# Linear attention and a multiplicative FFN on one core: another order of the steps, with the fold products begun in pairs

## The chip, the cores and the metric

One core of a Trainium2 chip runs the program. The metric is the device time of one execution in microseconds. Five engines work side by side, each on its own list of instructions in program order: TensorE (PE; its weight loads are shown apart as PEld), VectorE (DVE), ScalarE (ACT), GpSimd (POOL) and SyncE (SP). Transfers run in DMA queues. In this kernel GpSimd and SyncE issue nearly all of them; only the very last is issued by ScalarE.

## The reference, cut to what matters

```python
B, H, S, D = 8, 8, 576, 64              # q, k, v: float32

def phi(x):
    return np.where(x > 0, x, np.exp(x) - 1.0) + 1.0
q_p, k_p = phi(q), phi(k)
kv  = np.einsum('bhsd,bhse->bhde', k_p, v)
z   = np.sum(k_p, axis=2)
num = np.einsum('bhsd,bhde->bhse', q_p, kv)
den = np.einsum('bhsd,bhd->bhs', q_p, z)[..., None] + 1e-06
x   = (num / den).transpose(0, 2, 1, 3).reshape(4608, 512)

a = x @ w1                              # w1, w2: 512 x 1024
b = x @ w2
h = (a * b) @ w3                        # w3: 1024 x 1024
out = h @ w_out                         # w_out: 1024 x 512
```

## The kernel before

**Stages.** The kernel first folds the two last weights into one, wf = w3 @ w_out (eight row blocks i of 128; each is a sum of eight products of 512 columns, kc = 0 to 7). Then the attention runs batch by batch and fills xt, the transposed x, in bf16. The 4608 tokens are nine chunks c of 512. For each chunk eight column blocks f of a and b are computed (four products each, accumulated in PSUM), ScalarE copies a to SBUF, VectorE multiplies it with b to ab, and four products O of 128 tokens (eight matmuls of 512 columns each, against wf) give the output rows. Batches 0 and 1 use a path on TensorE alone for the transposes (q transposes and "first" products), batches 2 to 7 transpose q and x with DMAs of SyncE.

**The order.** Everything is a step in one text, `ORDER` (lines 19 to 68), and `step` (L486) carries the steps out one after the other under a manual schedule. The order in the text is therefore the order on each engine. Waits between engines follow from the data, and from the buffers of the pools: a new tile of a full pool waits until the oldest tile's last reader is done. A "+" at the end of a step puts it on the other engine: a copy on VectorE where it is on ScalarE otherwise, a load in GpSimd's queue where it is in SyncE's otherwise.

| step | what it does | line |
|---|---|---|
| lq, lk, lv b.part | load q, k or v of batch b (part 2: the whole of it) | L165 |
| lw x.y | load a piece of w1 (x = 0) or w2 (x = 1) | L171 |
| lo x | load a quarter of w_out: the rows for kc = 2x and 2x+1 | L181 |
| le i | load block i of w3 | L191 |
| i0, i1, i2, i3 | identity; ones and constants; zero tile; zeros into kvb, on GpSimd | L137 to L147 |
| H n | n products of the zero tile, into a PSUM tile of mm_ps | L152 |
| wt i, wc i | eight transposes of w3's block i on TensorE; their copy out | L202, L206 |
| wm i.k0.k1 | the fold products kc = k0 to k1-1 of block i | L212 |
| wd i | copy of the finished block into wf_sb | L216 |
| x, y, z with k or q | exp (ACT), linear part (DVE) and minimum (DVE) of phi | L226 to L237 |
| vc, K, kc, Z, kz | v's cast, k'v products and their copies, sums of k | L243 to L361 |
| T b.u | q's transpose as a DMA of SyncE | L274 |
| A, G, D | products q kv, their division (DVE), x's transpose as a DMA of SyncE | L286 to L320 |
| qa, qb, e, er, em, rm, rd | the same for batches 0 and 1 without DMA | L330 to L415 |
| g c.f.w.h | products of a (w = 0) or b (w = 1) of chunk c, block f; h = 2: all four kc, 0 or 1: one half | L428 |
| fc, fm c.f | copy of a (ACT), product a * b (DVE) | L439, L448 |
| O, oc c.m | output products of 128 tokens; their copy to an o_sb buffer | L456, L460 |
| S c.m | the store of that buffer, two DMAs of 128 KB (64 tokens each); GpSimd, for chunk 8 SyncE | L468 |
| Q 8.3 | the last output block in two parts, with copies and stores | L479 to L481 |

PSUM has four accumulators of the tag mm (fold products, a, b and O, L117) and two of the tag at (transposes, attention). The copies of O share six o_sb buffers:

```python
        o_sbs[c, m] = sm.tile([P, DM], F32, tag="o_sb", name="o_sb", bufs=6)
        copy_of(alt)(out=o_sbs[c, m], in_=o_pss[c, m])
```

so a copy oc waits until the store of the sixth oc before it has landed. In the text a store S stands some steps behind its copy; in between, the buffer is taken.

The front of the text before, to the first fold products, and the place where chunk 2's output products stand:

```
i2 lq0.0 H12 le3 le0 i0 le4 le1 lo1 xq0.0 yq0.0 lo0 lo2 wt3 lo3 H3 lk0.0+ wt0 le6 wc0+ lk0.1+ wc3+ wt4 zq0.0
le2 wt1 wc4+ lq0.1+ wc1+ qa0.0 le5 wm1.0.4 wm3.0.4 lk1.1+ wm4.0.4 le7 wm3.4.8 wm4.4.8 xk0.0 yk0.0 wm0.0.4
...
fm2.3 fm2.0 S0.1 G3.1 O2.2 oc1.3 D3.0 O2.1 oc2.2 vc5.0+ D3.1 vc4.1 yq4.1 lq5.2 O2.0 oc2.1 zq4.0 S2.2 vc4.0
```

Of the kernel before, what the change touches and what calls it, by code (L numbers as in the profile page):

```python
# [24 lines left out]
e0.1.1 kz0.0.0+ K0.1 er0.1.1 e0.0.0 kz0.0.1+ wm7.0.4 em0.0.0 wm7.4.8 em0.0.1 er0.1.0 wd5+ rm0 lw1.2 e0.1.0
g0.5.0.0 wd7 em0.1.1 g0.4.0.0 rd0 lv1.0+ em0.1.0 g0.0.0.0 g0.1.0.0 g0.0.0.1 lv1.1+ g0.5.0.1 fc0.0 g0.1.0.1
fc0.5 g0.6.0.0 lq2.2+ g0.6.0.1 fc0.1 yk1.0 g0.1.1.0 fc0.6 g0.1.1.1 lv2.2+ g0.4.0.1 xk1.0 fm0.1 g0.2.0.0
g0.2.0.1 fc0.4 g0.7.0.0 zk1.0 lk2.2+ g0.7.0.1 xq1.0 zk1.1 g0.0.1.0 g0.3.0.0 yq1.0 g0.3.0.1 fc0.7 g0.0.1.1
zq1.0 xq1.1 Z1.0 Z1.1 fm0.0 qa1.0 fc0.3 g0.3.1.0 qb1.0+ kz1.1.1 g0.2.1.0 kz1.1.0 g0.3.1.1 yq1.1 fc0.2 e1.0.1
g0.2.1.1 er1.0.1 zq1.1 g0.4.1.0 g0.5.1.0 fm0.2 g0.5.1.1 er1.0.0 fm0.3 g0.4.1.1 g0.7.1.0 fm0.5 g0.7.1.1 qa1.1  # L30
fm0.7 g0.6.1.0 qb1.1 g0.6.1.1 fm0.4 K1.0 fm0.6 K1.1 kz1.0.0 e1.1.1 kz1.0.1 e1.0.0 O0.3 er1.1.1 em1.0.1
em1.0.0 er1.1.0 e1.1.0 oc0.3+ O0.0 em1.1.1 S0.3 xq2.0 em1.1.0 g1.1.0.0 xq2.1 lk3.2 yq2.1 g1.7.0.0 g1.4.0.0
yq2.0 oc0.0 g1.7.0.1 g1.4.0.1 zq2.1 g1.1.0.1 fc1.4 g1.4.1.0 zq2.0 fc1.7 g1.7.1.0 g1.7.1.1 vc2.0+ T2.1 fc1.1
rm1 vc2.1 g1.1.1.0 fm1.7 g1.1.1.1 yk2.0 g1.3.0.0 xk2.1 T2.0 g1.3.1.0 fm1.1 g1.3.0.1 g1.4.1.1 yk2.1 fc1.3
g1.6.1.0 rd1 g1.0.0.0 fm1.4 lq3.2 g1.3.1.1 g1.0.0.1 xk2.0 fm1.3 lv3.2 g1.6.1.1 g1.6.0.0 zk2.1 fc1.0 g1.6.0.1
g1.0.1.0 zk2.0 fc1.6 lk4.2 g1.5.0.0 fm1.6 K2.0 K2.1 g1.0.1.1 kc2.1 kc2.0+ g1.5.1.0 fm1.0 A2.0 A2.1 g1.2.1.0
G2.0 g1.2.0.0 g1.5.0.1 g1.5.1.1 fc1.5 g1.2.1.1 g1.2.0.1 fm1.5 D2.0 A2.3 fc1.2 A2.2 O0.2 yq3.1 xq3.1 fm1.2
xk3.0 G2.1 O0.1 O1.1 oc0.1 yk3.0 D2.1 xk3.1 zq3.1 O1.2 lq4.2 xk4.1 oc1.1+ zk3.0 xq3.0 A2.4 yq3.0 g2.4.0.2
yk3.1 lv5.2 g2.5.0.2 fc2.4 zq3.0 g2.5.1.2 fc2.5 G2.2 T3.1 oc1.2 g2.7.0.2 oc0.2 yk4.1 g2.4.1.2 fc2.7 vc3.0+
# [5 lines left out]
T4.0 fc3.1 zk5.0 g3.4.0.2 vc5.1+ g3.3.0.2 fc3.4 S2.0 xq5.1 fm3.4 g3.5.0.2 yq5.1 g3.2.0.2 S2.3 fc3.5 yq5.0
g3.1.1.2 xq5.0 zq5.1 D2.2 g3.5.1.2 fm3.1 S1.2 K4.0 K4.1 fm3.5 fc3.2 g3.0.1.2 kc4.0 kc4.1+ fc3.3 zq5.0 A4.1
A4.0 g3.2.1.2 G4.0 T5.0 g3.0.0.2 g3.3.1.2 fm3.2 K5.0 D4.0 K5.1 fm3.3 fc3.0 g3.6.1.2 S1.3 kc5.0 fm3.0 A4.2
g3.7.1.2 kc5.1+ S2.1 A4.3 fm3.7 g3.6.0.2 T5.1 G4.1 fc3.6 g4.2.0.2 g4.2.1.2 fc4.2 lv6.2 g4.5.0.2 fm4.2 lq6.2
g4.3.0.2 fm3.6 fc4.5 g4.0.0.2 fc4.3 lk6.2 O3.1 fc4.0 A5.0 oc3.1+ O3.0 A5.1 oc3.0 g4.1.0.2 G5.0 S3.1 g4.5.1.2
vc6.0 D4.1 g4.0.1.2 fm4.5 g4.3.1.2 fm4.0 fc4.1 D5.0 g4.6.0.2 xq6.1 fm4.3 A4.4 g4.6.1.2 G4.2 fc4.6 g4.7.1.2  # L50
xq6.0 yq6.0 O3.3 lq7.2 yq6.1 xk6.0 fm4.6 g4.1.1.2 lk7.2 xk6.1 oc3.3+ A5.4 O3.2 fm4.1 S3.3 G5.2 D4.2 g4.7.0.2
oc3.2 zq6.0 g5.7.0.2 vc6.1+ fc4.7 g5.4.0.2 yk6.1 fc5.7 A5.2 D5.2 fm4.7 fc5.4 g4.4.0.2 zq6.1 g4.4.1.2 fc4.4
zk6.1 T6.1 xq7.0 g5.3.0.2 fm4.4 g5.3.1.2 xq7.1 yq7.0 O4.2 T6.0 yq7.1 fc5.3 zq7.0 xk7.1 O4.3 fm5.3 S3.2 oc4.2
yk7.1 xk7.0 S4.2 zq7.1 g5.7.1.2 zk7.1 oc4.3 g5.2.0.2 S4.3 fm5.7 g5.2.1.2 fc5.2 yk7.0 g5.6.0.2 S3.0 fm5.2
g5.5.1.2 fc5.6 zk7.0 lv7.2 g5.4.1.2 yk6.0 A5.3 g5.0.0.2 fm5.4 T7.1 zk6.0 O4.1 fc5.0 G5.1 T7.0 g5.0.1.2
g5.5.0.2 fm5.0 K6.0 fc5.5 oc4.1+ K6.1 D5.1 g5.6.1.2 kc6.1 fm5.5 kc6.0 S4.1 g5.1.1.2 vc7.0 fm5.6 A6.2 A6.3
vc7.1 g5.1.0.2 G6.1 O4.0 fc5.1 fm5.1 D6.1 A6.0 K7.0 K7.1 oc4.0+ O5.1 kc7.0 S4.0 kc7.1 A6.1 oc5.1 O5.3 G6.0
S5.1 O5.0 oc5.3+ D6.0 A7.4 oc5.0+ A7.1 S5.3 O5.2 G7.2 S5.0 A7.0 oc5.2 g6.4.0.2 G7.0 D7.2 g6.3.1.2 fc6.4 S5.2
g6.0.0.2 D7.0 g6.1.0.2 fc6.0 g6.0.1.2 fc6.1 g6.4.1.2 fm6.0 g6.2.0.2 fm6.4 g6.1.1.2 fc6.2 g6.6.1.2 fm6.1
g6.3.0.2 g6.7.0.2 fc6.3 fm6.3 g6.2.1.2 fc6.7 g7.2.0.2 fm6.2 g6.6.0.2 fc7.2 g7.7.0.2 fc6.6 fm6.6 g7.3.0.2  # L60
fc7.7 g7.2.1.2 g6.7.1.2 fm7.2 g7.6.1.2 fc7.3 fm6.7 g6.5.1.2 g7.6.0.2 g7.4.0.2 fc7.6 fm7.6 g7.7.1.2 fc7.4
g6.5.0.2 fm7.7 g7.3.1.2 fc6.5 fm6.5 g7.0.1.2 fm7.3 O6.1 O6.0 oc6.1+ S6.1 A7.3 oc6.0 g7.4.1.2 S6.0 g7.0.0.2
fm7.4 A6.4 fc7.0 O6.2 G6.2 fm7.0 D6.2 A7.2 g7.5.0.2 oc6.2+ g7.1.0.2 G7.1 S6.2 fc7.5 g7.5.1.2 fc7.1 g7.1.1.2
fm7.5 D7.1 O6.3 fm7.1 O7.2 oc6.3+ S6.3 g8.4.0.2 oc7.2 g8.3.0.2 S7.2 fc8.4 g8.7.0.2 fc8.3 g8.3.1.2 fc8.7
# [534 lines left out]
```

## Time and profile before

| | |
|---|---|
| time, median of 3 runs | 245.5 us (244.54 to 245.67) |
| the profiled execution's own time | 244.84 us |
| its span in the profile | 243.1 us |
| TensorE busy | 232.2 us, 96% of the span |
| VectorE, ScalarE, GpSimd busy | 148.9, 118.4 and 60.2 us |
| moved by DMA | 49.20 MB, 202 GB/s over the span |

The profile comes from one execution. Its span begins with the first and ends with the last recorded work, and the rest of that execution's own time, 1.74 us, lies around it. A row names the engine, the line, the instruction and the tiles it writes and reads (out<-in); times are in us, with the time from the span's start first where a row tells of one instruction. "<-" gives what released the engine after an idle time. The page divides the span into 40 slices; TensorE's row there begins with 8, 5 and 7, ends with 3, and is 9 in all slices between.

### The profile page before, as it was taken

To read this page: it belongs to the slowest core of one execution; us is meant where nothing else is said; L and a number is where in the kernel's file an instruction comes from. 1 tells how busy PE (TensorE), PEld (TensorE's weight loads), DVE (VectorE), ACT (ScalarE), POOL (GpSimd) and SP (SyncE) were. 2 spreads that over 40 slices of the span, in tenths; PEclk is the share of its full clock that TensorE was granted. 3 is DMA by queue.
4 is the path that set the end of the run, shared out by engine and by line. 5 is a ranking of instruction groups with operands and counts; after the bars stand their busy time and mean duration, and the time that the engine had idled before them with its cause. 6 is when DMAs were issued, how large, how long until landed. Compare 5 with 4: busy or idle time off the path is not lost.

```text
span 243.1 us, 4808 instructions
## 1 busy us (share of the span) xinstructions
PE 232.2 (96%) x1938; PEld 112.1 (46%) x1955; DVE 148.9 (61%) x280; ACT 118.4 (49%) x177; POOL 60.2 (25%) x104
## 2 busy tenths in 40 slices
...
GB/s 151 194 283 325 213 255 296 294 387 299 186 395 200 370 263 332 205 272 275 105 256 381 216 373 152 293 122 151 155 119 1 0 3 86 97 86 46 43 79 137
DMA packets 48470, 49.20 MB, mean 202 GB/s; under 512 B 30528, under 2 KB 34880, under 8 KB 48448
## 3 DMA queue, kind: packets, MB, share of 16 engines
...
q8 instruction: 15, 0.25, 0.4%
q10 hardware_dynamic: 144, 0.10, 0.1%
...
## 4 chain that ended last, share of the span: by engine, by line
PE 89%; DMA 4%; DVE 2%; ACT 1%; POOL 1%; issue 1%; POOLq 0%
PE b_ps L428 25%; PE o_ps L456 25%; PE a_ps L428 24%; PE wf_ps L212 6%; DMA wo<-in_moe_w_out_dram 4%; PE nd L286 3%; PE kvp L261 2%; POOL w3b L191 1%; PE w3p L202 1%; PE o_ps L479 1%; PE nd L372 1%; PE tq L330 1%; PE zp L349 1%; DVE k L237 1%; DVE ab L448 1%
## 5 line engine op out<-in xcount | busy, mean ns | idle before, releaser
L428 PEld LDWEIGHTS <-w_sb 128*128 128x128 bf16 x576 | 54.9, 98 | 63.9 <-issue 1.4
L468 POOL DMA_DIRECT2D out_dram<-o_sb x64 | 36.3, 571 | 157.1 <-ACT o_sb L460 72.8
L428 PE MATMUL b_ps<-xt,w_sb 128*128 128x512 bf16 x288 | 70.7, 379 | 0.0
L428 PE MATMUL a_ps<-xt,w_sb 128*128 128x512 bf16 x288 | 69.5, 379 | 0.4 <-DVE xt L392 0.3
L439 ACT COPY a_sb<-a_ps 128x512 f32<-128x512 f32 x72 | 41.7, 585 | 57.6 <-PE a_ps L428 41.6
L456 PE MATMUL o_ps<-wf_sb,ab 128*128 128x512 bf16 x266 | 63.2, 379 | 0.8 <-issue 0.2
L448 DVE TENSOR_TENSOR ab<-a_sb,b_ps 128x512 bf16<-128x512 f32 x64 | 45.8, 730 | 27.7 <-PE b_ps L428 17.8
L456 PEld LDWEIGHTS <-ab 128*128 128x128 bf16 x280 | 26.7, 98 | 31.0 <-issue 0.5
L460 ACT COPY o_sb<-o_ps 128x512 f32<-128x512 f32 x23 | 13.3, 585 | 38.4 <-PE o_ps L456 31.5
L226 ACT ACTIVATE e<-k 128x1152 bf16<-128x1152 f32 x16 | 18.3, 1161 | 12.3 <-DMA k<-in_k_dram 12.3
L226 ACT ACTIVATE e<-q 128x1152 bf16<-128x1152 f32 x16 | 18.4, 1163 | 2.4 <-DMA q<-in_q_dram 2.4
L212 PE MATMUL wf_ps<-wo,w3t 128*128 128x512 bf16 x61 | 14.7, 379 | 1.6 <-DMA wo<-in_moe_w_out_dram 1.3
L230 DVE TENSOR_SCALAR r<-k 128x1152 bf16<-128x1152 f32 x16 | 11.9, 749 | 6.1 <-DMA k<-in_k_dram 6.1
L308 DVE TENSOR_TENSOR xn<-nd,r 128x512 bf16<-128x512 f32 x24 | 15.4, 683 | 0.0
L230 DVE TENSOR_SCALAR r<-q 128x1152 bf16<-128x1152 f32 x16 | 12.5, 804 | 3.3 <-DMA q<-in_q_dram 3.3
L446 DVE TENSOR_TENSOR ab<-a_sb,b_ps 128x512 bf16<-128x512 f32 x8 | 5.5, 686 | 14.1 <-PE b_ps L428 9.4
L460 DVE COPY o_sb<-o_ps 128x512 f32<-128x512 f32 x12 | 8.3, 690 | 9.3 <-PE o_ps L456 9.0
L237 DVE TENSOR_TENSOR k<-e,r 128x1152 bf16<-128x1152 bf16 x16 | 11.8, 752 | 0.6 <-ACT e L226 0.5
L237 DVE TENSOR_TENSOR q<-e,r 128x1152 bf16<-128x1152 bf16 x16 | 11.8, 749 | 0.3
L286 PEld LDWEIGHTS <-qt 128*128 128x128 bf16 (+1 forms) x120 | 8.6, 100 | 7.2 <-issue 2.7
L286 PE MATMUL nd<-kvb,qt 128*128 128x130 bf16 (+1 forms) x120 | 11.2, 222 | 0.0
L212 PEld LDWEIGHTS <-w3t 128*128 128x128 bf16 x64 | 5.8, 98 | 8.2 <-DVE w3t L206 1.3
...
## 6 DMA issues: line engine op xcount, KB each, us to landing
...
```

Source lines behind the costliest of these rows:

```text
L212: nc.tensor.matmul(wfs[i], w3ts[i][:, kc, :], wos[0][:, kc, :], start=(kc == 0), stop=(kc == FC - 1))
L226: nc.scalar.activation(out=es[name, b, c], in_=raw[name, b][:, 2 * c:2 * c + 2, :], func=AF.Exp)
L230: nc.vector.tensor_scalar(out=rs[name, b, c], in0=raw[name, b][:, 2 * c:2 * c + 2, :], scalar1=0.0, scalar2=1.0, op0=ALU.max, op1=ALU.add)
L237: nc.vector.tensor_tensor(out=ph[name, b][:, c].rearrange("p j a d -> p a j d"), in0=es[name, b, c].rearrange("p a (j d) -> p a j d", j=NJ ...
L286: nc.tensor.matmul(nd[0:n, u, 2 * c * (D + 1):2 * (c + 1) * (D + 1)], w, kvb[b % 2][:, u, c].rearrange("p a e -> p (a e)"), start=True, st ...
L308: nc.vector.tensor_tensor(out=dst.rearrange("p (i u) e -> p u i e", u=2), in0=v4[:, :, :, 0:D], in1=r[0:n].unsqueeze(3).to_broadcast([n, 2 ...
L428: nc.tensor.matmul(fps[c, f, w], (w1_sb, w2_sb)[w][:, kc, f * P:(f + 1) * P], xt[:, 4 * c:4 * c + 4, kc, :], start=(first and n == 0), sto ...
L439: nc.scalar.copy(out=fsb[c, f], in_=fps[c, f, 0])
L448: nc.vector.tensor_tensor(out=abs_[c][:, f].rearrange("p (m t g) -> p m g t", g=2, t=R), in0=fsb[c, f].rearrange("p (m g t) -> p m g t", g ...
L456: nc.tensor.matmul(o_pss[c, m], abs_[c][:, f, m * P:(m + 1) * P], wf_sb[:, f, :], start=(f == 0), stop=(f == FC - 1))
L460: copy_of(alt)(out=o_sbs[c, m], in_=o_pss[c, m])
L468: queue.dma_start(out=out[bb * S:(bb + 1) * S, :].rearrange("(p j) n -> p j n", j=NJ)[:, j, :], in_=o_sbs[c, m][part])
```

## The change

The diff touches `ORDER` alone. It has one line more, so every later line number rises by one. The kinds of step and the functions stay.

- Each first half of a fold product, `wm i.0.4`, is now two steps of two matmuls, `wm i.0.2 wm i.2.4`. `wm i.4.8` stays.
- Zero products: H12 and H3 become H12, H4, H3 and H1, 15 to 20 in all.
- i3, the zeros into kvb on GpSimd, moves from behind yq0.1 to a place between le1 and lo1.
- The loads of the front have another order: le4 le0 le3 lo0 le1 lo1 le6 lo2 lo3 lk0.0 le2 lk0.1 lq0.1 le5 lv0.0, where it was le3 le0 le4 le1 lo1 lo0 lo2 lo3 lk0.0 le6 lk0.1 le2 lq0.1 le5 lk1.1.
- All other steps are in a new order too. Some copies change their engine: among others oc0.3 goes to ScalarE, oc7.0, oc7.1 and the oc8 to VectorE.
- Stores: S0.2, S6.0 and S3.3 stand at the very end, S1.0 behind K7.1, S0.0 and S1.2 among chunk 2's output products.

The text has 792 steps, where it had 782.

```diff
 ORDER = """
-i2 lq0.0 H12 le3 le0 i0 le4 le1 lo1 xq0.0 yq0.0 lo0 lo2 wt3 lo3 H3 lk0.0+ wt0 le6 wc0+ lk0.1+ wc3+ wt4 zq0.0
-le2 wt1 wc4+ lq0.1+ wc1+ qa0.0 le5 wm1.0.4 wm3.0.4 lk1.1+ wm4.0.4 le7 wm3.4.8 wm4.4.8 xk0.0 yk0.0 wm0.0.4
-wm1.4.8 qb0.0 zk0.0 wt6 i1 wd1 wm0.4.8 wc6+ xk0.1 yk0.1 wm6.0.4 wd3 lv0.0+ zk0.1 wt2 Z0.0 wd0 lv0.1+ wd4+
-Z0.1 wc2 wm6.4.8 lw0.2 kz0.1.0+ kz0.1.1+ xq0.1 lw0.0 wm2.0.4 yq0.1 i3 e0.0.1 wt5 zq0.1 er0.0.1 lw1.0 wm2.4.8
+i2 lq0.0 H12 le4 le0 le3 i0 lo0 le1 xq0.0 yq0.0 i3 i1 lo1 wt4 zq0.0 le6 H4 lo2 wt0 lo3 H3 wc0+ lk0.0+ wc4+
+wt3 le2 wc3+ qa0.0 lk0.1+ wm0.0.2 qb0.0 wm3.0.2 wm4.0.2 lq0.1+ wt1 H1 wc1+ le5 wm0.2.4 wm3.2.4 wm4.2.4
+lv0.0+ wm1.0.2 wm1.2.4 wt6 lv0.1+ le7 wm4.4.8 wm0.4.8 wc6+ wd4 lw0.0 yk0.0 wm3.4.8 xk0.0 wd0+ wm6.0.2
+wm6.2.4 zk0.0 wm6.4.8 xk0.1 yk0.1 wt2 wm1.4.8 lk1.1+ wc2+ wd3 lw0.2 zk0.1 wm2.0.2 xq0.1 wm2.2.4 lq1.0+ yq0.1
...
-fm2.3 fm2.0 S0.1 G3.1 O2.2 oc1.3 D3.0 O2.1 oc2.2 vc5.0+ D3.1 vc4.1 yq4.1 lq5.2 O2.0 oc2.1 zq4.0 S2.2 vc4.0
-zq4.1 A3.4 yk5.0 O2.3 T4.1 xk5.1 yk5.1 xk5.0 G3.2 g3.7.0.2 oc2.0 g3.1.0.2 zk5.1 D3.2 fc3.7 g3.4.1.2 oc2.3+
+D2.2 G3.1 xk5.1 O2.0 oc1.0 xk4.0 D3.1 O2.2 oc2.0+ zq4.0 S2.0 xq5.1 O2.1 yk4.0 T4.0 S0.0 zk4.0 yq5.1 S1.2
+O2.3 T4.1 yk5.1 oc1.3 K4.0 K4.1 oc2.2+ g3.1.0.2 lq6.2 kc4.0 S2.2 zq5.1 g3.4.0.2 oc2.3 S1.1 A3.4 fc3.4
+g3.5.0.2 G3.2 fc3.1 g3.1.1.2 S1.3 vc5.1 kc4.1+ D3.2 g3.4.1.2 fm3.1 S2.3 oc2.1 A4.1 fm3.4 g3.2.0.2 xq5.0 A4.0
...
+K7.1 S1.0 O4.0 kc7.0 kc7.1+ fm5.1 S4.1 fm5.3 T7.0 A6.0 oc4.0 A6.1 O5.3 G6.0 O5.0 oc5.3 D6.0 O5.2 oc5.0+ S5.0
...
-fc8.0 fm8.0 O8.0 oc7.3 S7.3 O8.1 oc8.0 S8.0 O8.2 oc8.1 S8.1 oc8.2 S8.2 Q8.3
+g8.3.1.2 fc8.5 fm8.5 g8.4.0.2 O7.1 fc8.4 fm8.4 fm8.3 O7.0 oc7.1+ S7.1 O7.2 oc7.0+ S3.3 O8.1 oc7.2 S7.2 O8.0
+S7.0 S0.2 O8.2 oc8.0+ oc8.1+ S6.0 S8.1 O7.3 oc8.2+ S8.2 oc7.3 S8.0 S7.3 Q8.3
```

More of the change, by code (lines that the diff above doesn't have):

```diff
@@ L25 @@
[L25 to L39, printed above, removed]
@@ L40 @@
-T3.0 g2.7.1.2 xq4.0 fm2.5 g2.2.0.2 vc3.1 zk3.1 g2.1.1.2 fm2.7 fc2.2 lv4.2 K3.0 K3.1 g2.1.0.2 kc3.1+ lk5.2
-fm2.4 g2.0.0.2 fc2.1 S0.2 kc3.0 fm2.1 g2.3.0.2 xq4.1 yk4.0 g2.6.0.2 S1.1 zk4.1 fc2.0 g2.2.1.2 fc2.6 yq4.0
-A3.0 xk4.0 g2.6.1.2 fm2.2 A3.1 O1.0 G3.0 g2.3.1.2 oc1.0 zk4.0 fc2.3 g2.0.1.2 S1.0 fm2.6 A3.3 A3.2 S0.0 O1.3
-fm2.3 fm2.0 S0.1 G3.1 O2.2 oc1.3 D3.0 O2.1 oc2.2 vc5.0+ D3.1 vc4.1 yq4.1 lq5.2 O2.0 oc2.1 zq4.0 S2.2 vc4.0
-zq4.1 A3.4 yk5.0 O2.3 T4.1 xk5.1 yk5.1 xk5.0 G3.2 g3.7.0.2 oc2.0 g3.1.0.2 zk5.1 D3.2 fc3.7 g3.4.1.2 oc2.3+
@@ L45 @@
[L45 to L64, printed above, removed]
@@ L65 @@
-g8.7.1.2 fm8.3 O7.0 fm8.7 g8.2.1.2 oc7.0 g8.2.0.2 S7.0 g8.6.0.2 fc8.2 fm8.2 g8.1.0.2 fc8.6 O7.1 fc8.1
-g8.5.0.2 oc7.1 g8.4.1.2 S7.1 g8.5.1.2 fm8.4 g8.0.1.2 fc8.5 fm8.5 g8.6.1.2 g8.1.1.2 fm8.6 g8.0.0.2 fm8.1 O7.3
-fc8.0 fm8.0 O8.0 oc7.3 S7.3 O8.1 oc8.0 S8.0 O8.2 oc8.1 S8.1 oc8.2 S8.2 Q8.3
+i2 lq0.0 H12 le4 le0 le3 i0 lo0 le1 xq0.0 yq0.0 i3 i1 lo1 wt4 zq0.0 le6 H4 lo2 wt0 lo3 H3 wc0+ lk0.0+ wc4+
+wt3 le2 wc3+ qa0.0 lk0.1+ wm0.0.2 qb0.0 wm3.0.2 wm4.0.2 lq0.1+ wt1 H1 wc1+ le5 wm0.2.4 wm3.2.4 wm4.2.4
@@ new lines @@
+lv0.0+ wm1.0.2 wm1.2.4 wt6 lv0.1+ le7 wm4.4.8 wm0.4.8 wc6+ wd4 lw0.0 yk0.0 wm3.4.8 xk0.0 wd0+ wm6.0.2
+wm6.2.4 zk0.0 wm6.4.8 xk0.1 yk0.1 wt2 wm1.4.8 lk1.1+ wc2+ wd3 lw0.2 zk0.1 wm2.0.2 xq0.1 wm2.2.4 lq1.0+ yq0.1
+Z0.0 Z0.1 lw0.1 kz0.1.0 kz0.1.1+ e0.0.1 zq0.1 wt5 er0.0.1 lw1.0 wm2.4.8 wc5+ er0.0.0 qa0.1 wd2+ lk1.0+
+wm5.0.2 qb0.1+ wm5.2.4 wd1 K0.0 lw1.1 K0.1 kz0.0.0+ e0.1.1 kz0.0.1 wt7 er0.1.0 wm5.4.8 wc7+ lq1.1+ e0.1.0
+er0.1.1 e0.0.0 wm7.0.2 em0.0.0 lw1.2 wm7.2.4 em0.0.1 wm7.4.8 wd6 em0.1.0 wd5 g0.1.0.0 rm0 xk1.1 em0.1.1
@@ new lines @@
+g0.0.0.0 lq2.2+ yk1.1 g0.1.0.1 g0.0.0.1 fc0.1 wd7+ g0.4.0.0 lv1.0+ g0.6.0.0 xq1.0 zk1.1 g0.5.0.0 g0.6.0.1
+yq1.0 lv1.1+ g0.5.0.1 fc0.6 g0.4.0.1 zq1.0 fc0.5 g0.3.0.0 lv2.2+ g0.3.0.1 fc0.0 g0.2.0.0 fc0.4 g0.1.1.0
+g0.1.1.1 fc0.3 g0.0.1.0 yk1.0 xk1.0 g0.0.1.1 g0.2.0.1 fm0.1 qa1.0 rd0 lk2.2+ zk1.0 g0.2.1.0 g0.2.1.1 qb1.0+
+Z1.0 xq1.1 g0.7.0.0 fm0.0 Z1.1 yq1.1 kz1.1.0 fc0.2 e1.0.1 g0.7.0.1 kz1.1.1+ er1.0.1 zq1.1 g0.6.1.0 g0.6.1.1
+fm0.2 g0.7.1.0 fc0.7 g0.7.1.1 fm0.6 er1.0.0 g0.5.1.0 g0.5.1.1 fm0.7 g0.3.1.0 fm0.5 g0.4.1.0 xq2.1 qa1.1
```

32 lines of the change are left out of this document (31 added, 1 removed).

## The prediction, made before the changed kernel was run

> **What bounds the kernel now.** I read the page first, then the chain that ended last in order of time, then TensorE's own waits.
>
> ```profile
> span 243.1 us, 4808 instructions
> PE 232.2 (96%) x1938; PEld 112.1 (46%) x1955; DVE 148.9 (61%) x280; ACT 118.4 (49%) x177; POOL 60.2 (25%) x104
> PE 89%; DMA 4%; DVE 2%; ACT 1%; POOL 1%; issue 1%; POOLq 0%
> ```
> ```profile
> 4.59 9.12 DMA wo<-in_moe_w_out_dram
> 13.76 0.38 PE wf_ps L212
> ...
> 141.99 2.59 PE a_ps L428 x12
> ...
> 161.45 0.71 PE kvp L261 x72
> ...
> 237.55 1.76 PE o_ps L479 x16
> 239.34 0.32 ACT o_sb L480
> ```
> ```profile
> PE w3p L202 <- DMA w3b<-in_moe_w_dram: 2.6, 3, 1.1
> PE wf_ps L212 <- DMA wo<-in_moe_w_out_dram: 1.3, 1, 1.3
> PE warm L152 <- DVE zero L144: 1.2, 1, 1.2
> PE a_ps L428 <- DVE xt L392: 0.3, 1, 0.3
> PE kvp L261 <- DVE kvz L361: 0.2, 1, 0.2
> PE nd L372 <- ACT kvz L361: 0.2, 1, 0.2
> ```
>
> The reader is to see one engine. From 13.76 us, when a piece of w_out lands, TensorE works without a break to 239.3 us; its named waits after that add up to 0.7 us. A product of 512 columns costs 2.59 / 12 = 0.216 us. The change leaves all products as they are, so it can gain only ahead of 13.76 us, in those 0.7 us, and behind the last product, and it loses whatever new wait its order puts on TensorE.
>
> **The front.** At most eight of GpSimd's DMAs are open: the ninth, and each later one, waits for the landing of the one eight before. So GpSimd's issue times give the landings, about 0.25 us earlier.
>
> ```profile
> 7.48 0.72 POOL L165 DMA_DIRECT2D k<-in_k_dram  x1 [1.08 <-DMA w3b<-in_moe_w_dram]
> ...
> 11.53 0.56 POOL L191 DMA_DIRECT2D w3b<-in_moe_w_dram  x1 [0.63 <-DMA w3b<-in_moe_w_dram]
> 12.75 0.72 POOL L165 DMA_DIRECT2D q<-in_q_dram  x1 [0.67 <-DMA wo<-in_moe_w_out_dram]
> 14.00 0.56 POOL L191 DMA_DIRECT2D w3b<-in_moe_w_dram  x1 [0.53 <-DMA wo<-in_moe_w_out_dram]
> 15.31 0.72 POOL L165 DMA_DIRECT2D k<-in_k_dram  x1 [0.76 <-DMA wo<-in_moe_w_out_dram]
> 16.55 0.56 POOL L191 DMA_DIRECT2D w3b<-in_moe_w_dram  x1 [0.52 <-DMA wo<-in_moe_w_out_dram]
> ```
> ```profile
> 17.74 0.76 DVE L230 TENSOR_SCALAR r<-k 128x1152 bf16<-128x1152 f32 x1 [5.09 <-DMA k<-in_k_dram]
> ...
> 35.71 2.32 PE L428 MATMUL a_ps<-xt,w_sb 128*128 128x512 bf16 x10 [0.32 <-DVE xt L392]
> ```
>
> Landings 4, 6, 7, 8 and 9 are thus at 11.3, 13.75, 15.05, 16.3 and 17.7 us, one each 1.25 to 1.4 us, whatever their order. Before, lo0 is the sixth. After, it is the fourth, and a step of two products needs lo0 alone: the three wm.0.2 steps (6 x 0.216 = 1.3 us) run from 11.3 us in time that was idle. Then the gift is paid back. lo1 is the sixth again (13.75), so the next six products start where the old ones did; then come four of wm1, wt6 (landing 7), two of wm4 (landing 8), and the next two need lo3, which is now the ninth: 17.6. By then the old order has done (17.6 - 13.76) / 0.216 = 17.8 products, the new one 18 and wt6's transposes (0.45): a lead of 0.5 us. lk0.1 is the twelfth instead of the eleventh, 1.2 us later; wc2 stands behind yk0.1 on VectorE, and wm2 waits for wc2. I take 0.3 us of the lead for what reaches the first f product; the bounds are the whole 1.3 us and a loss of 0.4 (that 1.2 us later minus the lead and the wm1.4.8 products, 0.86, that stand between). The five further zero products (H4, H1) stand in waits for le0 and lo1 and cost nothing; without that cover they cost 5 x 0.216 = 1.1 us. The kvb memsets (i3), now between le1 and lo1 on GpSimd, delay an issue whose data has 7 us to wait in the queue: nothing.
>
> At 35.7 us TensorE waits 0.3 us for xt. After, wm7's eight products stand between e0.1.0 and the f products, so VectorE has 1.7 us more. I take -0.3; from -0.7 (all named waits) to +0.4, as the new order has as many steps that follow their copy closely.
>
> **The stores.** S0.2 moves from soon after its copy to the very end, S3.3 and S6.0 there too; S1.0 goes to O4.0. Each holds one of the six o_sb buffers that long, so others are reused at once. Around O2 these waits stand in the program:
> - oc1.3 (ScalarE) waits for both halves of S2.0, and g3.1.0.2 needs the accumulator that it empties;
> - oc2.2 (VectorE) for S0.0; g3.4.0.2 needs it, and S2.2 is issued only after it;
> - oc2.3 for S1.2; g3.5.0.2 needs it;
> - oc2.1 for S2.2; g3.2.0.2 needs it.
>
> ```profile
> L460 ACT COPY o_sb<-o_ps 128x512 f32<-128x512 f32 x23 | 13.3, 585 | 38.4 <-PE o_ps L456 31.5
> ...
> L460 DVE COPY o_sb<-o_ps 128x512 f32<-128x512 f32 x12 | 8.3, 690 | 9.3 <-PE o_ps L456 9.0
> ```
> ```profile
> L468 POOL DMA_DIRECT2D out_dram<-o_sb x16: 534/540/548, 201.4 to 233.8; - x16
> DMA to landing us min/median/max: 1.9/2.0/2.0
> ```
> ```profile
> L468 POOL DMA_DIRECT2D out_dram<-o_sb x6: 534/540/548, 95.6 to 98.3; - x6
> DMA to landing us min/median/max: 2.6/2.9/3.5
> ```
> ```profile
> L468 POOL DMA_DIRECT2D out_dram<-o_sb x10: 534/546/946, 106.7 to 112.3; - x10
> DMA to landing us min/median/max: 3.3/4.2/4.8
> ```
> ```profile
> L468 POOL DMA_DIRECT2D out_dram<-o_sb x6: 534/542/931, 150.9 to 154.6; - x6
> DMA to landing us min/median/max: 2.9/3.8/5.0
> ```
> ```profile
> L468 POOL DMA_DIRECT2D out_dram<-o_sb x2: 678/841/1004, 101.2 to 102.2; - x2
> DMA to landing us min/median/max: 8.0/8.4/8.7
> ```
> ```profile
> 100.71 0.54 SPq L165 DMA_DIRECT2D q<-in_q_dram  x1
> 101.53 2.19 SPq L274 DMA_TRANSPOSE qt<-q  x1
> ...
> 106.52 3.17 SPq L274 DMA_TRANSPOSE qt<-q  x1
> ```
>
> Let L be the time from the issue of a half store to its landing, and count from O2.0's last product. oc2.0 takes 0.69 us on VectorE, with 0.2 to its start; S2.0's halves go out at 0.95 and 1.5, S0.0's at 2.05 and 2.6, S1.2's at 3.15 and 3.7 (0.54 each). TensorE meanwhile does O2.2, O2.1, O2.3 (24 x 0.216) and K4 (0.71): g3.1.0.2 is due at 5.9, and needs 1.5 + L + 0.7. That holds to L = 3.7. g3.4.0.2 is due at 6.8 and needs 2.6 + L + 0.8: L up to 3.4; g3.5.0.2 (7.9) likewise 3.5. S2.2 follows oc2.2, so its second half goes out at 3.95 + L, and oc2.1 is done at 4.65 + 2L; g3.2.0.2 is due at 10.7. From L = 3.0 on, TensorE stands still for 2L - 6.05 us there, the earlier waits included.
>
> What is L? The q transposes T4.0 and T4.1 go out from 1.5 us on, with lq6 behind them. An undisturbed store (2.0) costs nothing; xn transposes alone give 2.9; q transposes 4.2; q transposes beside a load 3.8; behind a load and a q transpose 8.4. The stage is nearest to the rows of 3.8 and 4.2, because T4 is first and the load comes later: I take L = 4.0, so +2.0 us. Bounds: 0 (L at 3.0 or less) and 3.8 us (L = 4.9).
>
> The Trainium skill's page "DMA: Bandwidth & Descriptors", section "Anatomy of one DMA — SWDGE (gpsimd) path", fits a GpSimd DMA at about 2.0 us plus bytes / 436 GB/s: for 128 KB about 2.3 us, an estimate from that page; by it the four waits cost nothing and the sum would be 2.0 us less. The trace agrees for the end of the kernel (2.0) and not for busy stages (2.9 to 8.4), so I go by the rows.
>
> Other reuses are looser: around O3, O4 and O5 the store has 3.6 us or more and the next product another 0.5 to 5; around O6, 2.6 us where the trace shows 2.0. I add nothing; up to 1 us if a load is in the way.
>
> **The end.** Order of products: O7.1, O7.0, O7.2, O8.1, O8.0, O8.2, O7.3, Q8.3, each O 1.73 us. GpSimd's seven late stores (1.08 us each) are done with S6.0 some 3.5 us ahead of the last product; S7.3 goes out about 1 us ahead and lands about 2 us behind it (2.0 above). Q8.3's second part is copied (0.32) and stored after it, as before, and ends later still. Nothing; if S7.3 were last, 0.5 us.
>
> **The sum.** Front -0.3, wait for xt -0.3, stores +2.0, rest 0: +1.4 us. Against the profiled execution (244.84: the span of 243.1 and 1.74 around it) that is 246.2; it lies 0.66 below the median of the runs shown, 245.5, on which the same sum gives 246.9. I say 246.5.
>
> **The rivals.**
> - *The stores land in time* (L about 2.9, as at 95.6 us, where two transposes were also under way). Against it: those were xn transposes. Then -0.6 remains: 244.2 to 244.9. Chance 0.27; the page's 2.3 us leads here as well.
> - *The lead is kept* as well: no paying back for lo3 and lk0.1, and all of TensorE's waits gone: 1.3 + 0.7 less, 242.8 to 243.5. For it: 1.3 us of products do move into idle time. Against it: landings 6 to 12 come at the same times, and the work behind them is the same. 0.12.
> - *lq6 is in the way*: the stores land as at 101.2 us (8.4). From L = 5 it passes my range; at 8.4 it is 10.7 us: 249 to 255. Against it: lq6 is issued behind both transposes. 0.08.
> - *The split does nothing*, because the first six products only wait for lo1 later: front 0, stores as forecast: 247; counted with the forecast.
>
> The forecast has 0.53. Half a per cent, 1.2 us, is about what a measurement of this kernel can tell from no change. The forecast's own range is 245.2 to 248.6 (L from 3.4 to 4.9), of which most lies over 246.7: slower 0.40, same 0.13. The stores in time are "same" but for 0.03; the lead kept is faster. Faster 0.15, same 0.37, slower 0.48. The range of 244.0 to 248.7 leaves out the lead kept and lq6 in the way.
>
> **What would show it.** The first wf product near 11.3 us; a wait of TensorE for lo3 near 17 us; the first f product within 0.5 us of 33.5. Around O2, ScalarE's and VectorE's o_sb copies released by DMA out_dram, half stores that take 3.4 us or more, and two or three gaps on TensorE ahead of a_ps of chunk 3, 2 us in all. It is wrong if those copies are released by o_ps, if the gaps stand elsewhere (a qt or xt transpose that lands late), or if the span ends with a store of GpSimd.

## The result, and the profile after

The changed kernel took 255.6 us (median of 4 runs, 255.11 to 258.12) where the kernel before took 245.57: a ratio of 1.0439, 95% interval 1.0363 to 1.0515. That is slower than the whole range forecast. The profiled execution took 256.04 us.

The page of the changed kernel, its first lines and its chain of waits:

```profile
span 254.3 us, 4822 instructions
PE 234.0 (92%) x1944; PEld 112.9 (44%) x1960; DVE 148.7 (58%) x280; ACT 118.3 (47%) x177; POOL 59.2 (23%) x104
PE 67%; DMA 19%; POOL 4%; issue 3%; ACT 3%; DVE 1%; DVEq 0%; ACTq 0%; POOLq 0%
```

TensorE's work is the same but for the five zero products (234.0 us busy, 232.2 before). The chain that ended last is no longer nearly all TensorE's: DMAs hold 19% of the span on it. It ends with ScalarE's last copy at 245.7 us and shows nothing of what comes behind that. The clock took no part: the granted clock was 1.00 from 0 to 245 us. TensorE's own waits, in us in total, times, longest:

```profile
PE a_ps L429 <- ACT o_sb L461: 3.7, 3, 2.3
...
PE a_ps L429 <- DVE o_sb L461: 1.1, 1, 1.1
PE nd L373 <- ACT kvz L362: 1.0, 2, 0.6
PE wf_ps L213 <- DMA wo<-in_moe_w_out_dram: 0.9, 2, 0.6
PE a_ps L429 <- DMA xt<-xn: 0.8, 1, 0.8
```

The first two shown, 4.8 us, are the waits around O2: products of a that need an accumulator which a copy to o_sb empties. TensorE's row over that stretch (start, length, what released it) shows the four places:

```profile
106.59 1.02 PE L429 MATMUL a_ps<-xt,w_sb 128*128 128x512 bf16 x4 [0.18 <-ACT o_sb L461]
108.66 1.02 PE L429 MATMUL a_ps<-xt,w_sb 128*128 128x512 bf16 x4 [1.05 <-DVE o_sb L461]
...
111.24 1.02 PE L429 MATMUL a_ps<-xt,w_sb 128*128 128x512 bf16 x4 [1.20 <-ACT o_sb L461]
...
116.50 1.02 PE L429 MATMUL a_ps<-xt,w_sb 128*128 128x512 bf16 x4 [2.27 <-ACT o_sb L461]
```

The copies in turn wait for stores. In the waits of the window from 98 to 118 us:

```profile
ACT o_sb L461 <- DMA out_dram<-o_sb: 11.1, 3, 4.8
...
DVE o_sb L461 <- DMA out_dram<-o_sb: 3.1, 1, 3.1
```

The four gaps are 4.7 us of TensorE's time. Its work ends 6.0 us later than before, and the end of the program 11.2 us later, so 5.2 us more are lost behind the last product. What stands there shows in a view that the prediction did not read: the instructions of the line that closes the program, L594 before and L595 after, where each engine has some (their count, duration in ns as least, median and most, first and last start in us). A DRAIN is one of them; the longest of GpSimd's three is its first. First the last rows of GpSimd and TensorE in the timeline of before, and the closing line of before:

```profile
233.29 1.07 POOL L468 DMA_DIRECT2D out_dram<-o_sb  x2 [6.70 <-ACT o_sb L460]
```
```profile
237.39 1.91 PE L479 MATMUL o_ps<-wf_sb,ab 128*128 128x320 bf16 x16
```
```profile
L594 POOLq DRAIN  x3: 46/93/8569, 233.7 to 242.8; - x3
L594 SPq DRAIN  x3: 7/7/7, 242.1 to 242.5; - x3
```

The same views of the changed kernel:

```profile
244.51 1.07 POOL L469 DMA_DIRECT2D out_dram<-o_sb  x2 [2.63 <-ACT o_sb L461]
```
```profile
243.43 1.91 PE L480 MATMUL o_ps<-wf_sb,ab 128*128 128x320 bf16 x16
```
```profile
L595 POOLq DRAIN  x3: 46/93/8569, 244.9 to 254.0; - x3
L595 SPq DRAIN  x3: 7/7/7, 249.2 to 253.8; - x3
```

GpSimd's first closing DRAIN takes 8.57 us in both. It begins with GpSimd's last half store, and it is over 7.9 us behind the end of that instruction (234.36 before, 245.58 after). Before, it ran from 233.7 to 242.3, and SyncE had its last landing at 242.1; it cost next to nothing. After, S7.3 is the last store and goes out at the very end: the drain runs from 244.9 to 253.5, while SyncE is done at 249.2. The end of the program is now GpSimd's.

### The profile page after: what moved, and what is told of

Same layout as the page of the kernel before. It is cut to its first block, busy times and chain, and to the rows that moved or that the text cites. A ratio compares the mean times of both kernels' runs of the same rounds, so it can differ in the third digit from the quotient of the medians.

```text
span 254.3 us, 4822 instructions
## 1 busy us (share of the span) xinstructions
PE 234.0 (92%) x1944; PEld 112.9 (44%) x1960; DVE 148.7 (58%) x280; ACT 118.3 (47%) x177; POOL 59.2 (23%) x104
## 4 chain that ended last, share of the span: by engine, by line
PE 67%; DMA 19%; POOL 4%; issue 3%; ACT 3%; DVE 1%; DVEq 0%; ACTq 0%; POOLq 0%
PE a_ps L429 21%; PE b_ps L429 21%; PE o_ps L457 18%; DMA k<-in_k_dram 5%; DMA v<-in_v_dram 4%; DMA out_dram<-o_sb 4%; DMA wo<-in_moe_w_out_dram 4%; PE nd L287 2%; DMA xt<-xn 2%; POOL out_dram L469 2%; PE kvp L262 1%; POOL w3b L192 1%; PE o_ps L480 1%; DVE o_sb L461 1%; PE nd L373 1%
## 5 line engine op out<-in xcount | busy, mean ns | idle before, releaser
L429 PE MATMUL a_ps<-xt,w_sb 128*128 128x512 bf16 x288 | 70.4, 379 | 5.5 <-ACT o_sb L461 3.7
L469 POOL DMA_DIRECT2D out_dram<-o_sb x64 | 35.6, 563 | 168.0 <-ACT o_sb L461 103.7
L429 PE MATMUL b_ps<-xt,w_sb 128*128 128x512 bf16 x288 | 70.0, 379 | 0.0
L440 ACT COPY a_sb<-a_ps 128x512 f32<-128x512 f32 x72 | 40.8, 588 | 57.0 <-PE a_ps L429 52.1
L449 DVE TENSOR_TENSOR ab<-a_sb,b_ps 128x512 bf16<-128x512 f32 x64 | 45.5, 730 | 30.8 <-PE b_ps L429 17.1
L457 PE MATMUL o_ps<-wf_sb,ab 128*128 128x512 bf16 x268 | 62.1, 379 | 0.6
L461 DVE COPY o_sb<-o_ps 128x512 f32<-128x512 f32 x11 | 7.5, 688 | 16.7 <-PE o_ps L457 8.4
L231 DVE TENSOR_SCALAR r<-k 128x1152 bf16<-128x1152 f32 x16 | 11.9, 754 | 3.0 <-DMA k<-in_k_dram 2.8
L305 DVE TENSOR_SCALAR r<-nd 128x8 f32<-128x8 f32 (+1 forms) x30 | 4.1, 159 | 14.6 <-PE nd L287 14.4
L238 DVE TENSOR_TENSOR q<-e,r 128x1152 bf16<-128x1152 bf16 x16 | 11.9, 750 | 0.6 <-ACT e L227 0.5
L287 PE MATMUL nd<-kvb,qt 128*128 128x130 bf16 (+1 forms) x120 | 10.4, 222 | 0.0
L244 ACT CAST vt<-v 128x1152 bf16<-128x1152 f32 x9 | 10.4, 1179 | 0.0
## 6 DMA issues: line engine op xcount, KB each, us to landing
k<-in_k_dram SPq DMA_DIRECT2D x5, 1152.0 KB, 10.3
q<-in_q_dram POOLq DMA_DIRECT2D x3, 576.0 KB, 11.2
```

Source lines behind the costliest of these rows:

```text
L231: nc.vector.tensor_scalar(out=rs[name, b, c], in0=raw[name, b][:, 2 * c:2 * c + 2, :], scalar1=0.0, scalar2=1.0, op0=ALU.max, op1=ALU.add)
L238: nc.vector.tensor_tensor(out=ph[name, b][:, c].rearrange("p j a d -> p a j d"), in0=es[name, b, c].rearrange("p a (j d) -> p a j d", j=NJ ...
L287: nc.tensor.matmul(nd[0:n, u, 2 * c * (D + 1):2 * (c + 1) * (D + 1)], w, kvb[b % 2][:, u, c].rearrange("p a e -> p (a e)"), start=True, st ...
L429: nc.tensor.matmul(fps[c, f, w], (w1_sb, w2_sb)[w][:, kc, f * P:(f + 1) * P], xt[:, 4 * c:4 * c + 4, kc, :], start=(first and n == 0), sto ...
L440: nc.scalar.copy(out=fsb[c, f], in_=fps[c, f, 0])
L449: nc.vector.tensor_tensor(out=abs_[c][:, f].rearrange("p (m t g) -> p m g t", g=2, t=R), in0=fsb[c, f].rearrange("p (m g t) -> p m g t", g ...
```

## The experiments

Two costs were suspected first: the copies around O2 and the drain. Each experiment changes the order text, unless said otherwise. The runs stand in several sessions, in which the kernel before had medians of 244.84 to 245.57 us; so a difference to the changed kernel, which ran in the first of them, is uncertain by some 0.7 us.

**e1_before_o73_last: the drain alone, put into the kernel before.**

```diff
-O7.3 fc8.0 fm8.0 O8.0 oc7.3 S7.3 O8.1 oc8.0 S8.0 O8.2 oc8.1 S8.1 oc8.2 S8.2 Q8.3
+fc8.0 fm8.0 O8.0 O8.1 oc8.0 S8.0 O8.2 oc8.1 S8.1 oc8.2 S8.2 O7.3 oc7.3 S7.3 Q8.3
```

> The kernel before with one edit: O7.3, its copy and its store stand between S8.2 and Q8.3 instead of ahead of O8.0 and O8.1, as in the changed kernel. TensorE's work is the same. Theory (GpSimd's closing drain): both traces end with a DRAIN on GpSimd of 8.57 us that starts with the last GpSimd store; here that store goes out some 5 us later, near 238.8 instead of 233.8, and the drain is no longer over together with SyncE's last landing: span about 248.1 and time +4.5 to +5.2 us over before. Rival (the prediction's own step, that a store 1 us ahead of the last product costs nothing): 0 to +0.5 us.

Measured: 251.82 us, +7.0 over before in the same session (244.84); ratio 1.0298 (1.0262 to 1.0335). GpSimd's last row in this run's timeline, and its closing drain:

```profile
239.40 1.07 POOL L468 DMA_DIRECT2D out_dram<-o_sb  x2 [13.45 <-ACT o_sb L460]
```
```profile
L594 POOLq DRAIN  x3: 46/102/8569, 239.8 to 248.9; - x3
```

The store moved from 233.3 to 239.4 us, and the span grew by the same 6.1 us (243.1 to 249.2), while TensorE's work ended 0.9 us later. The theory stands; the estimate missed that TensorE loses 0.9 us as well: without O7.3 in between, O8.0 waits 1.4 us for chunk 8's products ab.

**e2_after_s73_sync: S7.3 out of GpSimd's queue.**

```diff
-            queue = nc.sync if c == NT * P // NCH - 1 else nc.gpsimd
+            queue = nc.sync if c == NT * P // NCH - 1 or (c, m) == (7, 3) else nc.gpsimd
```

> The changed kernel with one edit: S7.3's two half stores are issued by SyncE instead of GpSimd. Theory (drain): the last GpSimd store is then S6.0's second half at 241.3; its drain ends near 249.8, and SyncE, with two issues more, near 250 to 250.5: 3.0 to 3.7 us less than the changed kernel. Rival (the last landing counts, and GpSimd doesn't): SyncE ends 1.2 us later, so +1.2 us.

Measured: 253.6 us (253.09 to 255.92), 2.0 below the changed kernel, not above it; the two profiled spans are 3.0 apart (251.3 and 254.3). In its profile the span ends 5.0 us behind TensorE instead of 9.0, and GpSimd's drain (241.7 to 250.6) is still the last to end. The sign speaks for the drain; between the medians the size is smaller than forecast. TensorE's work in that execution ended 0.9 us later, and it had a granted clock of 0.50 from 118 to 120 us and 0.72 from 120 to 122, where the changed kernel's was 1.00.

**e8_before_pool_copy: what the drain is counted from.** One GpSimd copy of a single column is added to the kernel before, behind the store of O8.2:

```diff
             o_store(x, y)
+            if (x, y) == (8, 2):
+                nc.gpsimd.tensor_copy(out=zero[:, 0:1], in_=o_sbs[8, 2][:, 0:1])
```

> The kernel before with one more GpSimd instruction at its end: a copy of one column of the o_sb buffer of O8.2 into the unused zero tile, behind S7.3, possible only near 238.5 us. The output is the reference's. It tells what the 8.57 us of the closing drain are counted from. Theory A (from GpSimd's last instruction, of any kind): the drain ends near 247.2 instead of 242.3, time +4 to +5 us. Theory B (from GpSimd's last DMA): drain shorter, about 4 us, time +0 to +0.7 us.

Measured: 248.82 us, +3.8 over before (245.0), ratio 1.0139 (1.0086 to 1.0193); the profiled span is 4.4 longer (247.5). GpSimd's last two rows in its timeline, and the closing drain:

```profile
233.70 1.07 POOL L468 DMA_DIRECT2D out_dram<-o_sb  x2 [6.70 <-ACT o_sb L460]
238.65 0.18 POOL L563 CAST zero<-o_sb 128x1 bf16<-128x1 f32 x1 [3.88 <-ACT o_sb L460]
```
```profile
L596 POOLq DRAIN  x3: 46/102/8139, 238.6 to 247.3; - x3
```

The last store is at nearly the same time (233.7 against 233.3), and still the drain lasts 8.14 us and begins with the copy. So theory A stands: it counts from GpSimd's last instruction, a store or a copy; other kinds were not tried. It is over 7.93 us behind the end of the 0.18 us copy, and in 15 of the 17 profiles 7.91 us behind the end of a last half store of 0.55 us (7.75 in e2): it is the end of the last instruction that counts. What GpSimd does in these 8 us, no run shows.

**e9_after_tail_only: the end of the changed kernel alone put right.**

```diff
-O7.1 fc8.4 fm8.4 fm8.3 O7.0 oc7.1+ S7.1 O7.2 oc7.0+ S3.3 O8.1 oc7.2 S7.2 O8.0
-S7.0 S0.2 O8.2 oc8.0+ oc8.1+ S6.0 S8.1 O7.3 oc8.2+ S8.2 oc7.3 S8.0 S7.3 Q8.3
+S3.3 S0.2 S6.0 O7.1 fc8.4 fm8.4 fm8.3 O7.0 oc7.1+ S7.1 O7.2 oc7.0 S7.0 O7.3 oc7.2+ S7.2
+O8.1 oc7.3 S7.3 O8.0 oc8.1+ S8.1 O8.2 oc8.0 S8.0 oc8.2+ S8.2 Q8.3
```

> The changed kernel with its end alone put right: S3.3, S0.2 and S6.0 go out ahead of O7.1, and the last products stand in the order O7.1 O7.0 O7.2 O7.3 O8.1 O8.0 O8.2 Q8.3 with each store behind its copy. The stores around O2 stay late. Theory (the two losses add up): TensorE's gaps between 104 and 117 us stay at 4.5 to 5, and the span ends 3.7 to 4 us behind TensorE instead of 9: time 4 to 5.5 us less than the changed kernel, 250 to 251.5. Rival (the GpSimd drain only grows with the stores that are still open, and another wait takes its place at the end): less than 2 us.

Measured: 252.56 us (250.04 to 252.8), 3.0 below the changed kernel. TensorE's gaps between 104 and 117 us are still there (waits for o_sb copies of 2.7 and 1.1 us, somewhat less than the 4.5 to 5 expected), and the end is whole again. TensorE's last row in the timeline, and the closing line:

```profile
245.34 1.91 PE L479 MATMUL o_ps<-wf_sb,ab 128*128 128x320 bf16 x16
```
```profile
L594 POOLq DRAIN  x3: 46/93/8571, 241.7 to 250.7; - x3
L594 SPq DRAIN  x3: 7/7/7, 250.2 to 250.5; - x3
```

GpSimd's drain (241.7 + 8.57 = 250.3) is over together with SyncE's (250.2), and the span of 251.0 ends 3.8 us behind TensorE's last product, as before the change. The mechanism is as forecast, and the gain of 3.0 lies below its 4 to 5.5. The profiled execution lost time elsewhere: its first f product came at 34.1 us instead of 32.9, and its granted clock was 0.50 from 112 to 114 us and 0.68 from 114 to 116. The one of the four runs with a clock of 1.00 took 250.04 us, inside the forecast.

**e3_after_8_buffers: eight o_sb buffers instead of six.** All three places that allocate the tag get `bufs=8`.

> The changed kernel with eight o_sb buffers instead of six. Theory (copies around O2 wait for the buffer of a late store): three of the four waits go, TensorE's 5 us of gaps between 104 and 117 us shrink to under 1, and the time is 4 to 5 us less than that of the changed kernel, near 251; the 4 us at the end stay. Rival (the stores and transposes are slow there in any case, and the copies wait for something else, ScalarE's or VectorE's queue): no change, 255 to 256.

Measured: 251.93 us (250.84 to 252.69), 3.7 below the changed kernel, a little less than forecast. No o_sb copy is left among TensorE's waits in its profile; two transposes are late instead:

```profile
PE a_ps L428 <- DMA xt<-xn: 1.3, 1, 1.3
...
PE nd L286 <- DMA qt<-q: 0.6, 1, 0.6
```

So the copies were held by buffers, as the theory has it.

**e4_after_lq6_late: the q load of batch 6 taken from among the stores.**

```diff
-O2.3 T4.1 yk5.1 oc1.3 K4.0 K4.1 oc2.2+ g3.1.0.2 lq6.2 kc4.0
-g3.5.0.2 G3.2 fc3.1 g3.1.1.2 S1.3 vc5.1 kc4.1+ D3.2 g3.4.1.2
+O2.3 T4.1 yk5.1 oc1.3 K4.0 K4.1 oc2.2+ g3.1.0.2 kc4.0
+g3.5.0.2 G3.2 fc3.1 g3.1.1.2 S1.3 vc5.1 kc4.1+ D3.2 lq6.2 g3.4.1.2
```

> The changed kernel with the load of q of batch 6 behind D3.2 instead of ahead of kc4.0. Theory (the q load is what makes S2.2's stores slow, 6 us where T4 alone leaves 4.5): they land in about 4 us, TensorE's third gap of 2.4 us shrinks to under 0.5: 2 us or more less than the changed kernel. Rival (q transposes and eight half stores in a row are slow by themselves): under 0.7 us less.

Measured: 252.78 us (252.46 to 254.83), 2.8 below the changed kernel. Three answers on the changed kernel, each one tile in a window (instructions and their starts, and the time to landing in us): the stores of the two bursts around O2, and the q load:

```profile
L469 POOL DMA_DIRECT2D out_dram<-o_sb x6: 534/609/1011, 101.5 to 104.9; - x6
...
DMA to landing us min/median/max: 2.3/4.2/5.6
```
```profile
L469 POOL DMA_DIRECT2D out_dram<-o_sb x8: 534/540/548, 108.9 to 112.6; - x8
...
DMA to landing us min/median/max: 5.4/6.0/6.5
```
```profile
L166 SPq DMA_DIRECT2D q<-in_q_dram x1: 1772/1772/1772, 106.8 to 106.8; - x1
...
DMA to landing us min/median/max: 8.5/8.5/8.5
```

The first burst, beside the q transposes, lands in 4.2 us at the median; the second, S2.2 first, goes out 2 us behind the load and takes 6.0. With the load moved, the first burst takes 4.5 at the median, and the second only 2.3:

```profile
L468 POOL DMA_DIRECT2D out_dram<-o_sb x8: 534/540/546, 109.6 to 113.3; - x8
...
DMA to landing us min/median/max: 2.0/2.3/7.5
```

So it was the load that made the second burst slow. TensorE's own waits for o_sb copies shrink to these two rows of that list:

```profile
PE a_ps L428 <- DVE o_sb L460: 1.6, 1, 1.6
...
PE a_ps L428 <- ACT o_sb L460: 0.2, 1, 0.2
```

The last and longest gap (2.27 us) is gone and the third (1.20 us) is down to 0.2, as this theory says.

**e5_after_stores_at_once and e6_at_once_o73_early.** In the first, every S stands directly behind its oc. The second has the order of the last products of e9 in addition.

> The changed kernel with every store S directly behind its copy in the text; all else in the same order. Theory (two separate costs, late buffers and GpSimd's late closing drain): the copies around O2 wait for no store, TensorE's gaps between 104 and 117 us go (under 0.3 us), its work ends near 240.5; S7.3 is still the last GpSimd store, 0.3 us ahead of TensorE's end, so the span ends 9 us behind that: span near 249.5, time near 251. Rival (once the stores are early, the end is early as well): span 244, time 245.5. Rival (the stall at O2 was the q load and transposes on ScalarE's and VectorE's own inputs): gaps of 2 us or more stay.

> The run before this one with, in addition, O7.3, its copy and its store moved ahead of O8.1, O8.0 and O8.2. Theory: S7.3's second half goes out some 5.3 us ahead of TensorE's end, so GpSimd's drain is over together with SyncE's last landing: 5 to 6 us less than the run before this one, 244.5 to 246, the same as the kernel before within 0.5%. Rival (the new order has another loss, not yet seen): over 247. Rival (the front's lead counts once the losses are gone): under 244.3.

Measured: 252.95 us (252.6 to 253.7) and 247.53 us (247.08 to 247.83). The 5.4 us between the two are the drain's, as forecast, and the gaps between 104 and 117 us are under 0.1. But both are 1.5 to 2 us slower than forecast, as e6's rival with a loss not yet seen has it, through a wait that was not there before. The load of k of batch 5 in the changed kernel (its line in a window), then in e6 the waits of that stretch and the same load:

```profile
L166 SPq DMA_DIRECT2D k<-in_k_dram x1: 368/368/368, 86.7 to 86.7; - x1
...
DMA to landing us min/median/max: 10.3/10.3/10.3
```
```profile
ACT e L226 <- DMA k<-in_k_dram: 4.6, 1, 4.6
...
PE o_ps L456 <- ACT o_sb L460: 1.8, 1, 1.8
```
```profile
L165 SPq DMA_DIRECT2D k<-in_k_dram x1: 679/679/679, 87.6 to 87.6; - x1
...
DMA to landing us min/median/max: 13.4/13.4/13.4
```

The load takes 13.4 us instead of 10.3 when stores of chunks 0 and 1 are sent at once; ScalarE waits 4.6 us for it, with an o_sb copy queued behind, and TensorE 1.8 us for that copy. How the stores delay the load is not shown: in the kernel before it took 8.7 us, although four half stores had gone out from 83.2 us on, 5 us ahead of it.

**e10_stores_as_before: four of these stores moved in the text to behind the loads.**

```diff
+S0.2 (behind fc2.0)  S1.1 (behind g2.6.0.2)  S1.2 (behind fc2.6)  S0.0 (behind fc2.3)
```

> The run with stores at once and O7.3 early, with four stores moved behind the loads of v and k of batch 5, about where the kernel before has them: S0.2 behind fc2.0, S1.1 behind g2.6.0.2, S1.2 behind fc2.6, S0.0 behind fc2.3. Theory (the 1.8 us gap at 101 us came from k of batch 5, which landed at 101.0 instead of 97.0 because eight half stores of chunks 0 and 1 were sent ahead of it and beside it): that load lands near 97, the gap is under 0.4 us, time 1.5 to 2 us less than that run, 245.2 to 246.2. Rival (the gap is that of ScalarE's order and stays): no change, 247.5.

Measured: 247.53 us, no change. The text doesn't hold a store back: GpSimd has its own list, and these stores went out as soon as their copies were done, still before and beside the load. GpSimd's row in this run's timeline, and the load:

```profile
82.94 3.57 POOL L468 DMA_DIRECT2D out_dram<-o_sb  x6 [2.26 <-ACT o_sb L460]
```
```profile
L165 SPq DMA_DIRECT2D k<-in_k_dram x1: 713/713/713, 87.9 to 87.9; - x1
...
DMA to landing us min/median/max: 13.1/13.1/13.1
```

In the kernel before, S0.2 and S1.1 go out at 83.2 us; then S1.0, whose copy comes late, stands at the head of GpSimd's list and keeps S0.0 and S0.1 back until 95.6. So the run doesn't tell the two theories apart as it was meant to; what it shows is that the load was late again.

**e11_8buf_lq6_tail: both costs mended together.** Eight buffers, the load behind D3.2, the end of e9, all other stores late as the change has them.

> The changed kernel with all its stores in chunks 0 to 6 left late, but eight o_sb buffers, the q load of batch 6 behind D3.2, and the end put right as in the run with that alone. Theory (three costs and no more: buffers, q load, drain): gaps at O2 under 0.5 us, end 3.8 us behind TensorE, 244.5 to 246. Rival (a transpose for xt or qt comes late once the stores are moved, as the 1.3 us at 177 us in the run with eight buffers): 246.5 to 247.5.

Measured: 246.44 us (246.29 to 246.97), ratio 1.0062 (1.0038 to 1.0087). That is 1.4 us over before in its own session (245.02), so about 8.6 of the 10.0 us lost are the stall at O2, for which two of the three edits stand, and the drain. Two rows of TensorE's own waits in its profile, both in the first third of the time:

```profile
PE zp L349 <- DVE k L237: 1.0, 1, 1.0
...
PE kvp L261 <- DVE vt L243: 0.6, 1, 0.6
```

**e13, e14: the new start with the old rest, and the reverse.** The two texts have the same steps done, but for fm1.2 and vc3.0, ahead of xq3.0 (after) and yq3.1 (before), so they can be joined there. In e14 the rest is that of e11.

> The changed kernel's order up to chunk 1's last product steps (as far as the step ahead of xq3.0, with the split fold products and the added zero products), and from there the order of the kernel before, with its stores and its end. It gives the price of the new start alone. Theory (the lead at the first f product is lost to k of batch 1, loaded two places later, and 0.5 to 1.3 us more is lost to waits between 42 and 64 us): +0.5 to +1.5 us over before. Rival (the new start is as good or better, and what was left in the run with eight buffers came from the rest): -0.5 to +0.3 us.

> The other way round: the start of the kernel before, then the changed kernel's order with eight buffers, the q load of batch 6 behind D3.2, and the end put right. Theory (all of the remaining loss stands in the start): the same as before within 0.4 us, 244.6 to 245.4, at best 0.3 below it. Rival (the new rest has a loss that TensorE's waits don't show): 245.8 or more.

Measured: 245.65 us, ratio 1.0025 (1.0006 to 1.0043), and 246.05 us, ratio 1.0028 (1.0005 to 1.0052). By these ratios the remainder is in both halves: 0.6 us in the start (interval 0.1 to 1.1), 0.7 us in the rest (0.1 to 1.3). The second theory, that all of it stands in the start, falls: the new rest, mended, still has waits for transposes. TensorE's own waits in e14:

```profile
PE nd L285 <- DMA qt<-q: 0.7, 1, 0.7
PE a_ps L427 <- DMA xt<-xn: 0.6, 1, 0.6
```

**e7, e15: the split of the fold products taken out**, of e6 and of e13. Each `wm i.0.2` goes and its `wm i.2.4` becomes `wm i.0.4`.

> The run before this one with the first halves of the fold products whole again: each wm i.0.2 is taken out and its wm i.2.4 becomes wm i.0.4. Theory (the split moves 1.3 us of products into idle time, and waits for later landings take it back): within 0.5 us of the run before this one, first f product within 0.4 us of it. Rival (the split's gain is real and was only hidden by the losses): 0.8 to 1.3 us slower than the run before this one.

> The first of these three with the first halves of the fold products whole again (each wm i.0.2 out, wm i.2.4 becomes wm i.0.4). Theory (the split is worth nothing, because the waits for loads behind it take back what it gains): within 0.5 us of the first of these three. Rival (the split gains its 1.3 us, or a part): slower than that by 0.7 us or more.

Measured: e7 248.48 us, ratio 1.0128 (1.0077 to 1.0180), against 1.0094 (1.0060 to 1.0129) of e6. The 0.95 us between them are what the rival forecast, but the intervals overlap and the two profiled spans are the same (245.7): nothing decided. e15 with ten runs settles it: 245.64 us, ratio 1.0024 (1.0005 to 1.0043), against 1.0025 with the split, and the first f product comes at 32.72 us without the split, at 32.76 with it. The split is worth nothing that these runs can tell.

**e12_no_extra_zero: H4 and H1 taken out of e10.**

> The run with four stores moved behind the loads, without the added zero products H4 and H1. Theory (they stand in waits for landings): within 0.4 us of that run. Rival (they are on TensorE's path): 0.8 to 1.1 us less.

Measured: 247.41 us against 247.53. The five further zero products cost nothing that these runs can tell.

No version that ran is faster than the kernel before.

## Why the prediction was wrong, step by step

- **What bounds the kernel**: right. In the profiles of the two kernels the time moved through waits of TensorE and through the end.
- **The front, -0.3 us**: right as far as it looked, and wrong in sign for the whole. The lead was there (first f product at 32.9 us instead of 33.5), with a wait for w_out near 17 us as forecast, but it isn't the split's (e15), and it was lost further back than the prediction looked. The first half of k of batch 1 is the 24th of GpSimd's loads instead of the 22nd. It is sent at 27.8 us in both kernels, but took 11.9 us instead of 8.8 and landed at 39.7 instead of 36.6, and TensorE waits 0.3 us in the sums of k ("PE zp" above, there up to 1.0). With 0.4 us for kvz at 44.7 us and 0.6 for vt at 64.0, that is more than the lead. e13 has +0.6 us for the whole new start, where this term and the next have -0.6. That the zero products cost nothing (e12) was right.
- **The wait for xt at 35.7 us, -0.3**: it is gone, as forecast, and others of its size stand behind it, those just named.
- **The stores, +2.0**: the mechanism was right, in all four places and in their order; the term was too small: 4.7 us. L was taken as 4.0 for all stores. That held for the first burst (median 4.2), not for the second (6.0), which stood behind the q load and took 2.3 without it (e4). With 4.2 and 6.0 in place of 2L, the prediction's own 2L - 6.05 gives 4.2, an estimate near the 4.7. The argument against the rival "lq6 in the way" was that the load goes out behind both transposes. It does, but S2.2 waits for S0.0 first, and so comes behind the load. Of the time that this rival was given (249 to 255), the stall is a part; its whole price of 10.7 us didn't come, since no store of the two bursts took more than 6.5. That the measured time lies so near to this rival's is chance, as 5.2 of the 11.2 us lost between the profiles are the drain's. The estimate by the Trainium skill's page "DMA: Bandwidth & Descriptors", section "Anatomy of one DMA — SWDGE (gpsimd) path", 2.3 us, agrees with the stores at the end (medians 2.0 us before, 2.1 after) and with none of the second burst. The 1 us allowed for another place came in part: TensorE waits 0.8 us for an xt transpose at 181 us.
- **The end, 0**: this step failed, and with it the range. "Lands about 2 us behind it ... Q8.3 ... ends later still" compared landings. The landings were about as said, but the end of GpSimd isn't its last landing: it is its drain, 8.57 us from its last store. "If S7.3 were last, 0.5 us" was that step's price for what came, and it cost 5.2. In the kernel before, the drain began at 233.7 us and was covered by SyncE's last landing; its row was in that trace, and the prediction did not look at the closing lines. Delaying GpSimd's last store by 11.2 us delayed the span by 11.2 us; with that store early enough the span would have ended some 3.8 us behind TensorE, as in e9.

The sum in the two profiles: 4.7 at O2, 0.8 at the xt transpose, about 0.5 elsewhere make TensorE's 6.0; 5.2 at the end make the 11.2 of the spans. Between the medians it is 10.0.
